# Fewer products on zeros at program begin, gate masks on GpSimd, diagonals and one V copy on VectorE

## The chip, the cores and the metric

One core of one Trainium2 chip. The metric is the device time of one execution in microseconds (us), lower is better. The profiled span leaves out some 1.75 us of it (for instance a span of 799.7 and a time of 801.38 for one execution).

## The reference

A layer-norm, an attention part in four segments of 512 rows, and a gated MLP over 2048 rows. Only the beginning of the first part matters here:

```python
x = A_x                                  # 1 x 2048 x 1024, bfloat16
h = x + A_ref(layernorm(x), wq, wk, wv, wo, beta)
h2 = h + B_ref(layernorm(h), w_in, w_sp, b_sp, w_out)

# inside A_ref, for each of 4 segments of 512 rows, 32 heads of width 32:
#   logits = q k^T * scale + causal mask; a_dot = softmax(logits) v
#   g = sigmoid(beta) per head; o = g * a_mem + (1 - g) * a_dot
#   M = M + phi(k)^T v; z = z + sum(phi(k))
```

## The kernel before

The kernel records operations for five engines and derives the semaphore waits from what each reads and writes. Each engine is given its own operations in the order recorded; loads are issued by SyncE in their order. The loads at the beginning:

```python
for tc in range(4):
    x_load(tc)                                  # 4 x 256 KB: the rows of segment 0
for i in range(0, 8, 2):                        # wv in four quarters of 256 KB
    sp.dma_start(WV[0][:, i:i + 2, :], A_wv[i * 128:(i + 2) * 128, 0:512]...)
sp.dma_start(WK[:, :, 0:256], ...)
sp.dma_start(WQ[:, :, 0:256], ...)
sp.dma_start(BETAB[:], A_beta.partition_broadcast(128))
sp.dma_start(WV[1][:], ...)
```

The first segment is normalised in a hurry: each tile of 128 rows is centred (its mean subtracted), transposed on TensorE, copied out of PSUM, and multiplied by the V weights; the row scale `RS0` is applied afterwards, when V is copied out of PSUM, and for Q and K by a product of ones with diagonal matrices (`DIAG`, a high and a low part). Until the first centred tile is there, TensorE multiplies zeros:

```python
def warm(k):
    for _ in range(k):
        pe.matmul(bank(7), IDENT[:], ETMP[:, 0, :], start=True, stop=True)   # ETMP is zero

def rstd0(tc):
    pool.tensor_tensor(RS0[tc][:], RS[tc][:, 0:1], MHALF[:], ALU.pow)
    pool.tensor_single_scalar(DIAG[0][:, tc, :], IDENT[:], RS0[tc][:], ALU.mult)

def diag_lo(tc):
    dve.scalar_tensor_tensor(DIAG[1][:, tc, :], IDENT[:], RS0[tc][:], DIAG[0][:, tc, :], ALU.mult, ALU.subtract)

warm(12)
act_mean(1)
var0(ln_stats(XCH[0]))
c0 = center(0, MV[0][:, 0:1], ALU.subtract)
c1 = center(1, MEAN[1][:])
pe_Th(0, c0, dve, dve)          # 8 transposes, two copies, both on VectorE
act_mean(2)                     # ACT: waits for x tile 2
pe_Th(1, c1, act, dve)          # 8 transposes, one copy on ACT, one on VectorE
# ... tiles 2 and 3 ...
warm(2)
for i in range(5):
    for t in range(2):
        v_mm(0, t, 0, vb[t], i)  # first V products: tiles 0 and 1 in turn, quarters of WV in order
# ...
mm8(bank(bk), lambda i: WK[:, i, 0:128], lambda i: XNT[0][:, i, :])
for i in range(2):
    pe.matmul(bank(br), ONES[:], DIAG[i][:]..., start=(i == 0), stop=(i == 1))
# ... rest of WK and WQ is loaded here (1.5 MB each) ...
gates()
phi_exp(0)
phi_max(0)                      # ends with a DMA transpose into PK
```

A quad is four heads. In the round of quad `n` TensorE does logits, projections of quad `n+1`, the products with V of quad `n-1`, and one product for the running state. The masks of the gates are made in the first round, on VectorE:

```python
def mask_g():
    dve.tensor_copy(MASKG[:, :, :, 0:32], GS[:]...to_broadcast([128, NQ, 4, 32]))
    for i in range(4):
        dve.tensor_single_scalar(MASKG[:, :, i, 0:32], MASKG[:, :, i, 0:32], BLK[:, i:i + 1], ALU.mult)
    for c in range(NQ):
        dve.tensor_copy(MASKG[:, c, :, 32], BLK[:])
# in the loop over rounds:  if n == 0: mask_g()
```

## Time and profile before

| | before |
|---|---|
| time, median of 3 | 802.42 us (802.40 to 802.46) |
| span of the profiled execution | 800.9 us |
| TensorE busy | 790.9 us |
| clock record at full speed from | 7.34 us |
| first V product | 8.41 us |
| first quarter of WV landed | 7.25 us |

The clock record is the trace's list of the clock granted to TensorE; in this trace products of 512 columns start 0.427 us apart before that instant and 0.216 us apart after it. "Landed" is the last of the 16 increments with which a load reports its parts.

The page's head and first part:

```profile
span 800.9 us, 12431 instructions
PE 790.9 (99%) x5304; PEld 380.8 (48%) x5374; DVE 380.5 (48%) x777; ACT 298.6 (37%) x348; POOL 127.3 (16%) x239
```

TensorE is the bound, so only what shortens its own order counts. The waits of TensorE in the first 34 us (what it waited for: us in total, times, longest):

```profile
PE ps L209 <- DVE ident L209: 1.7, 1, 1.7
PE ps L209 <- DVE rd L209: 0.5, 1, 0.5
PE ps L209 <- ACT e L209: 0.3, 2, 0.2
PE ps L209 <- issue: 0.2, 1, 0.2
```

("Issue" is time in which the profile shows nothing that was waited for.) The timeline of TensorE (start, us, engine, line, operation, output<-inputs, count, and in brackets the idle time before it with what ended it). Every operation has line 209, that of the recorder; one goes by tiles.

```profile
1.74 5.30 PE L209 MATMUL ps<-etmp,ident 128*128 128x512 bf16 x12 [1.74 <-DVE ident L209]
6.84 1.30 PE L209 MATMUL ps<-ident,lno 128*128 128x128 bf16 x16
7.98 0.59 PE L209 MATMUL ps<-etmp,ident 128*128 128x512 bf16 x2
8.41 2.32 PE L209 MATMUL ps<-wv,xnT 128*128 128x512 bf16 x10
...
16.21 0.59 PE L209 MATMUL ps<-diag,ones 128*128 128x512 bf16 x2
...
30.50 0.41 PE L209 MATMUL ps<-v,pk 128*128 128x132 bf16 x4
31.45 1.67 PE L209 MATMUL ps<-xnT,wq 128*128 128x512 bf16 x7 [0.54 <-DVE rd L209]
```

There is no idle bracket between 1.74 and 8.41: the products on zeros fill that time. At 31.45 there is one. VectorE's timeline says why it was late there, with 3.4 us on the masks:

```profile
25.44 0.72 DVE L209 COPY maskg<-gs 128x1024 f32<-128x1024 f32 x1
26.20 2.02 DVE L209 TENSOR_SCALAR maskg<-maskg,blk 128x256 f32<-128x256 f32 x4
28.25 0.67 DVE L209 COPY maskg<-blk 128x4 f32<-128x4 f32 x8
```

### The profile page before, as it was taken

How to read it: one execution, taken by the hardware profiler on the slowest of the kernel's cores; microseconds unless marked ns; L12 is line 12 of the kernel's file. 1: busy time of each engine (PE TensorE's matmuls, PEld its weight loads, DVE VectorE, ACT ScalarE, POOL GpSimd, SP SyncE). 2: the span in 40 equal slices, each digit the busy share in tenths (PEclk: the TensorE clock that was granted, in tenths of full speed). 3: DMA queues.
4: the chain of work that ended last, by engine and by line, in shares of the span. 5: the costliest groups of instructions: out<-in, count | busy, mean ns of one | idle time of the engine just before them, and what ended most of it. 6: DMA issues, size and time to landing. Idle time of an engine off the chain costs nothing.

```text
span 800.9 us, 12431 instructions
## 1 busy us (share of the span) xinstructions
PE 790.9 (99%) x5304; PEld 380.8 (48%) x5374; DVE 380.5 (48%) x777; ACT 298.6 (37%) x348; POOL 127.3 (16%) x239
## 2 busy tenths in 40 slices
PE   9999999999999999999999999999999999999998
PEld 4445445555444445455544444444444444444444
DVE  6875688569853774844562000063234323323432
ACT  5777877877778675133333333100000000000000
POOL 3443333233333331100131000000000000000000
PEclk9999999999999999999999999999999999999999
DMA  9672535353515324611117000650270153021003
GB/s 299 169 162 58 93 81 119 87 100 83 100 32 126 113 54 105 166 47 53 53 53 132 1 0 1 200 110 5 80 132 1 33 114 71 0 66 48 1 7 86
DMA packets 125000, 64.79 MB, mean 81 GB/s; under 512 B 94992, under 2 KB 113936, under 8 KB 124944
## 3 DMA queue, kind: packets, MB, share of 16 engines
q1 hardware_dynamic: 124944, 63.99, 33.3%
q8 instruction: 42, 0.69, 0.4%
q14 instruction: 14, 0.11, 0.0%
HBM read 32.51 MB, written 8.39 MB: 51 GB/s over the span
## 4 chain that ended last, share of the span: by engine, by line
PE 95%; DVE 4%; issue 1%; ACT 0%
PE ps L209 95%; DVE stats L209 1%; DVE maskg L209 0%; DVE ta L209 0%; DVE otok L209 0%; DVE hch L209 0%; DVE pqk L209 0%; ACT e L209 0%; DVE rd L209 0%; DVE lno L209 0%; DVE etmp L209 0%; DVE qk L209 0%; DVE mzb L209 0%; DVE rdm L209 0%; DVE msum L209 0%
## 5 line engine op out<-in xcount | busy, mean ns | idle before, releaser
L209 PE MATMUL ps<-wspT,z 128*128 128x512 bf16 x878 | 193.1, 379 | 0.9
L209 ACT ACTIVATE e<-ps 128x2048 bf16<-128x2048 f32 (+1 forms) x96 | 152.8, 1592 | 49.3 <-PE ps L209 48.8
L209 PEld LDWEIGHTS ps<-wspT,z 128*128 128x128 bf16 x896 | 87.7, 98 | 105.7
L209 DVE TENSOR_TENSOR tmpg<-ps,brow 128x512 f32<-128x512 f32 x56 | 38.7, 691 | 197.0 <-DMA brow<-in_B_b_sp_dram 105.5
L209 POOL TENSOR_SCALAR_AFFINE_SELECT e<-e 128x512 bf16<-128x512 bf16 x128 | 84.4, 671 | 185.4 <-ACT e L209 185.4
L209 PE MATMUL ps<-win,hnT 128*128 128x448 bf16 x512 | 98.3, 352 | 0.0
L209 PE MATMUL ps<-w_out,yT 128*128 128x512 bf16 (+2 forms) x453 | 96.9, 372 | 0.5
L209 PE MATMUL ps<-hnT,win 128*128 128x512 bf16 x439 | 96.2, 379 | 0.5
L209 PEld LDWEIGHTS ps<-win,hnT 128*128 128x128 bf16 x512 | 49.8, 98 | 46.3 <-issue 0.2
L209 PEld LDWEIGHTS ps<-w_out,yT 128*128 128x128 bf16 x462 | 44.7, 98 | 52.4
L209 PEld LDWEIGHTS ps<-hnT,win 128*128 128x128 bf16 x448 | 43.8, 98 | 52.8
L209 PE MATMUL ps<-xnT,wk 128*128 128x512 bf16 x256 | 60.8, 380 | 0.0
L209 PE MATMUL ps<-wv,xnT 128*128 128x512 bf16 x254 | 58.7, 379 | 0.2 <-issue 0.2
L209 ACT ACTIVATE z<-ps 128x448 bf16<-128x448 f32 x60 | 32.5, 543 | 69.4 <-PE ps L209 69.4
L209 PE MATMUL ps<-wo,oT 128*128 128x512 bf16 x254 | 57.6, 379 | 0.1
L209 ACT ACTIVATE z1T<-ps 128x512 bf16<-128x512 f32 x56 | 33.4, 597 | 63.3 <-PE ps L209 63.3
L209 PE MATMUL ps<-xnT,wq 128*128 128x512 bf16 x226 | 54.0, 379 | 2.1 <-DVE rd L209 0.5
L209 DVE TENSOR_TENSOR fin<-fin,ps 128x512 bf16<-128x512 bf16 (+2 forms) x33 | 22.2, 672 | 71.2 <-DMA fin<-out_dram 40.0
L209 DVE BATCH_NORM_STATS2 zst<-z 128x6 f32<-128x448 bf16 x64 | 38.9, 620 | 30.1 <-ACT z L209 30.1
L209 PEld LDWEIGHTS ps<-v,e 128*128 128x128 bf16 x1280 | 37.3, 96 | 9.1 <-issue 1.7
L209 DVE TENSOR_TENSOR yT<-tmpg,z1T 128x512 bf16<-128x512 f32 x56 | 38.8, 692 | 1.9
L209 PE MATMUL ps<-v,e 128*128 128x33 bf16 x1280 | 38.4, 177 | 0.0
(82 smaller groups left out, 577.1 us busy)
## 6 DMA issues: line engine op xcount, KB each, us to landing
xch<-in_A_x_dram SPq DMA_DIRECT2D x16, 256.0 KB, 3.3
xr<-in_A_x_dram SPq DMA_DIRECT2D x16, 256.0 KB, 3.4
out_dram<-hch SPq DMA_DIRECT2D x16, 256.0 KB, 2.5
fin<-out_dram SPq DMA_DIRECT2D x16, 256.0 KB, 2.8
out_dram<-fin SPq DMA_DIRECT2D x31, 128.0 KB, 1.7
win<-in_B_w_in_dram SPq DMA_DIRECT2D x4, 896.0 KB, 5.3
w_out<-in_B_w_out_dram SPq DMA_DIRECT2D x1, 3584.0 KB, 13.7
win<-in_B_w_in_dram SPq DMA_DIRECT2D x3, 1024.0 KB, 5.3
```

The lines of the kernel that those rows point to most:

```text
L209: ins = getattr(e, op.name)(*op.args, **op.kw)
```

## The change

The intent: three products on zeros fewer, so that the transposes start when the first centred tile is ready; the masks on GpSimd, so that VectorE is not late in the first round; the diagonals' high parts on VectorE, next to the low ones; one copy of V on VectorE, so that ACT's exponentials are not held up; beta loaded earlier, since the gates are now computed earlier.

```diff
     sp.dma_start(WK[:, :, 0:256], wcols(A_wk, 0, 256))
+    sp.dma_start(BETAB[:], A_beta.partition_broadcast(128))
     sp.dma_start(WQ[:, :, 0:256], wcols(A_wq, 0, 256))
-    sp.dma_start(BETAB[:], A_beta.partition_broadcast(128))
@@ mask_g
-        dve.tensor_copy(MASKG[:, :, :, 0:32], ...)
+        pool.tensor_copy(MASKG[:, :, :, 0:32], ...)
         for i in range(4):
-            dve.tensor_single_scalar(MASKG[:, :, i, 0:32], ...)
-        for c in range(NQ):
-            dve.tensor_copy(MASKG[:, c, :, 32], BLK[:])
+            pool.tensor_single_scalar(MASKG[:, :, i, 0:32], ...)
+        pool.tensor_copy(MASKG[:, :, :, 32], BLK[:].unsqueeze(1).to_broadcast([128, NQ, 4]))
@@ v_out
+        if (s, tcl, half) == (0, 3, 0):
+            dve.tensor_single_scalar(o, v, RS0[tcl][:], ALU.mult)
+        else:
+            act.activation(o, v, ACTF.Copy, scale=RS0[tcl][:] if s == 0 else 1.0)
@@ rstd0 and diag_lo
-        pool.tensor_single_scalar(DIAG[0][:, tc, :], IDENT[:], RS0[tc][:], ALU.mult)
-    def diag_lo(tc):
+    def diag(tc):
+        dve.tensor_single_scalar(DIAG[0][:, tc, :], IDENT[:], RS0[tc][:], ALU.mult)
         dve.scalar_tensor_tensor(DIAG[1][:, tc, :], ...)
@@ order
-    warm(12)
+    warm(9)
...
     proj_v(0, 2, 0)
+    gates()
+    mask_g()
     bk, bq, br = next_bank(), next_bank(), next_bank()
...
-    gates()
     phi_exp(0)
...
-        if n == 0:
-            mask_g()
```

More of the change, by code (lines that the diff above doesn't have):

```diff
@@ L426, in mask_g @@
     def mask_g():
-        dve.tensor_copy(MASKG[:, :, :, 0:32],
-                        GS[:].rearrange("p (c i) -> p c i", i=4).unsqueeze(3).to_broadcast([128, NQ, 4, 32]))
+        pool.tensor_copy(MASKG[:, :, :, 0:32],
+                         GS[:].rearrange("p (c i) -> p c i", i=4).unsqueeze(3).to_broadcast([128, NQ, 4, 32]))
         for i in range(4):
-            dve.tensor_single_scalar(MASKG[:, :, i, 0:32], MASKG[:, :, i, 0:32], BLK[:, i:i + 1], ALU.mult)
-        for c in range(NQ):
-            dve.tensor_copy(MASKG[:, c, :, 32], BLK[:])
+            pool.tensor_single_scalar(MASKG[:, :, i, 0:32], MASKG[:, :, i, 0:32], BLK[:, i:i + 1], ALU.mult)
+        pool.tensor_copy(MASKG[:, :, :, 32], BLK[:].unsqueeze(1).to_broadcast([128, NQ, 4]))
     lnc = [0]
@@ L475, in v_out @@
     def v_out(s, tcl, half, b):
-        act.activation(V[:, tcl, 16 * half:16 * half + 16, 0:32], bank(b).rearrange("p (h d) -> p h d", d=32),
-                       ACTF.Copy, scale=RS0[tcl][:] if s == 0 else 1.0)
+        o = V[:, tcl, 16 * half:16 * half + 16, 0:32]
+        v = bank(b).rearrange("p (h d) -> p h d", d=32)
+        if (s, tcl, half) == (0, 3, 0):
+            dve.tensor_single_scalar(o, v, RS0[tcl][:], ALU.mult)
+        else:
+            act.activation(o, v, ACTF.Copy, scale=RS0[tcl][:] if s == 0 else 1.0)
     def v_mm(s, tcl, half, b, i):
@@ L681, in bass_sequential_preLN__memory_aug_infini_attn__mixer_gmlp__prompt_kernel @@
     rstd0(2)
-    diag_lo(0)
+    diag(0)
     for i in range(5, 8):
@@ L687, in bass_sequential_preLN__memory_aug_infini_attn__mixer_gmlp__prompt_kernel @@
     v_out(0, 0, 0, vb[0])
-    diag_lo(1)
-    diag_lo(3)
-    diag_lo(2)
+    diag(1)
+    diag(3)
+    diag(2)
     v_out(0, 1, 0, vb[1])
     proj_v(0, 2, 0)
+    gates()
+    mask_g()
     bk, bq, br = next_bank(), next_bank(), next_bank()
```

## The prediction

> **What bounds it now.** TensorE is busy 790.9 of 800.9 us (page, busy times); 95% of the chain that ended last is TensorE. The change gains only what it takes out of TensorE's order before the steady state. In the timeline of 0 to 60 us three gaps do not recur:
>
> - Start: the first product on zeros starts at 1.74 us, the twelve follow every 0.427 us, the first transposes start at 6.83. The trace's clock record goes to full speed at 7.33: 512-column products are 0.427 us apart before, 0.216 after; transposes 0.107 and 0.056. The Trainium skill, "TensorE: Matmul & The Clock Gate", Part 1, gives these spacings (the trace agrees) and says that the window that opens the clock runs free and counts time, not products.
> - At 22.56 and 24.96 TensorE waits some 0.22 us each for ACT's exponentials (1.88 us) of quad 0.
> - At 31.45 the Q projection starts 0.71 us late, 0.22 in later rounds: 0.49 lost. It waits for VectorE's `qk`/`rd`, late because the gate masks take 3.4 us (25.44 to 28.9, VectorE's timeline).
>
> **The change, and its worth.**
>
> 1. Three products fewer: 3 x 0.427 = 1.28 us. The first centred tile is written at 5.63, so transposes start near 5.69, not 6.83. But if the clock still opens at 7.33, the 16 transposes now run cold (1.65 us; 1.14 before), and the first V product starts near 7.80, not 8.40. Worth 0.6. Quarters of WV land at 7.25, 8.09, 8.82, 9.59, needed from 7.8, 8.7, 9.5, 10.4.
> 2. Diagonals on VectorE. GpSimd's took 0.62 us each; the last diagonal ended at 16.10, TensorE used it at 16.20. Without this part the 0.6 would be lost there. VectorE needs about 0.25 + 0.35 us a pair (estimate from its low parts) and should end near 15.4; TensorE asks at 15.6. It protects (1), and is the tightest spot.
> 3. Masks on GpSimd: 3.4 us off VectorE; the 0.49 should vanish. GpSimd's affine select of 512 elements takes 0.65 us, so I estimate 3 to 6 us for 1024 + 4 x 256 + 32 elements, from 16.2 on. It idles until its selects (22.59), so nothing is held.
> 4. V copy on VectorE: ACT's second exponential started at 23.04, when its logits had just ended, so the copy hid in the wait. Worth about 0.
> 5. Beta ahead of WQ: 8 KB. WQ lands at 13.13, needed at 16.0. Worth 0.
>
> The DMA engines are saturated until about 28 us. The rest of WK lands at 24.7 (needed 26.7), the rest of WQ at 28.9 (needed 30.0), the first `pk` transpose at 29.3 (needed 29.8): little slack, but none should bind.
>
> **On the critical path:** 0.60 + 0.49 = 1.1 us; after 31 us every round takes 7.6 us of TensorE without a new wait, so the shift should reach the end. 802.42 - 1.1 = 801.3 us; 8 in 10: 800.6 to 801.9. Chances: faster by over 2% 0.01, within 2% 0.98, slower by over 2% 0.01.
>
> **What would show it.** (1) First V product near 7.8, first logits near 19.6 instead of 20.19, the clock record again at 7.3. (2) No wait before the `diag,ones` products. (3) The 0.71 spacing back to 0.22, GpSimd's masks over by 22 us. (4) ACT's exponentials at the same distance from the logits.
>
> **What would make it wrong.** The clock opens a window later (about 3.4 us) because the array idles at 5.6: loses up to 1.7 us. Or earlier: gains up to 1.2 instead of 0.6. Diagonals late, or VectorE and GpSimd slowing each other, would eat a few tenths. A load (rest of WQ, `pk`) that does not move earlier would cap the second gain.

## The result, and the profile after

Four executions of the changed kernel took 802.38, 801.76, 801.38 and 801.94 us, median 801.85; four of the kernel before on the same chip 802.40 to 802.46, median 802.43. The ratio is 0.9993, 95% interval 0.9976 to 1.001: the same. (Ratios are the mean time of one kernel's fast runs over that of the other's of the same rounds, so not quite the ratio of the medians quoted.) The median lies in the predicted range of 800.6 to 801.9, but only 0.05 us below its upper end, and two of the four executions lie above it; the gain is 0.6 us where 1.1 was forecast, and the changed kernel's executions differ by 1.0 us.

The profiled execution is the slowest of the four, 802.38 us. Its page, head and first part:

```profile
span 800.7 us, 12419 instructions
PE 789.3 (99%) x5301; PEld 380.0 (47%) x5371; DVE 379.2 (47%) x769; ACT 297.9 (37%) x347; POOL 129.0 (16%) x241
```

TensorE is busy for 1.6 us less, and the span is only 0.2 us shorter: it now waits. Its waits in the first 34 us:

```profile
PE ps L209 <- DVE ident L209: 1.7, 1, 1.7
PE ps L209 <- DMA wv<-in_A_wv_dram: 1.2, 1, 1.2
PE ps L209 <- DVE lno L209: 0.6, 1, 0.6
PE ps L209 <- ACT e L209: 0.3, 2, 0.2
```

Two waits are new; `rd` and the 0.2 us of "issue" are gone. Its timeline:

```profile
1.74 3.45 PE L209 MATMUL ps<-etmp,ident 128*128 128x512 bf16 x9 [1.74 <-DVE ident L209]
5.80 1.07 PE L209 MATMUL ps<-ident,lno 128*128 128x128 bf16 x16 [0.61 <-DVE lno L209]
6.70 0.59 PE L209 MATMUL ps<-etmp,ident 128*128 128x512 bf16 x2
8.51 2.32 PE L209 MATMUL ps<-wv,xnT 128*128 128x512 bf16 x10 [1.21 <-DMA wv<-in_A_wv_dram]
...
16.31 0.59 PE L209 MATMUL ps<-diag,ones 128*128 128x512 bf16 x2
...
30.78 0.41 PE L209 MATMUL ps<-v,pk 128*128 128x132 bf16 x4
31.24 1.67 PE L209 MATMUL ps<-xnT,wq 128*128 128x512 bf16 x7
```

The transposes start 1.04 us earlier than before, and the first V product 0.10 us later: it waits for the first quarter of WV, which landed at 8.37 us here and at 7.25 in the trace of before. The clock record reads full speed from 4.47 us, not 7.34. At 31.24 the bracket with `rd` is gone, as forecast. The masks on GpSimd took 5.6 us (16.35 to 21.97), inside the forecast, and GpSimd still idled before its first select:

```profile
16.35 1.05 POOL L209 COPY maskg<-gs 128x1024 f32<-128x1024 f32 x1 [2.00 <-DVE gs L209]
17.50 4.16 POOL L209 TENSOR_SCALAR maskg<-maskg,blk 128x256 f32<-128x256 f32 x4
21.73 0.24 POOL L209 COPY maskg<-blk 128x32 f32<-128x32 f32 x1
22.68 0.64 POOL L209 TENSOR_SCALAR_AFFINE_SELECT e<-e 128x512 bf16<-128x512 bf16 x1 [0.71 <-ACT e L209]
```

The chain of waits through the first 50 us (start, us, what) shows both loads that now hold TensorE. It runs through the quarter of WV, then TensorE, then the first transpose into `pk`:

```profile
2.65 5.72 DMA wv<-in_A_wv_dram
8.37 0.14 issue
8.51 3.63 PE ps L209 x22
...
20.49 10.24 DMA pk<-pqk
30.73 0.05 issue
30.78 0.41 PE ps L209 x4
```

The transpose's landing at 30.73 costs 0.20 us: the state products follow 0.53 us after the logits before them (30.25), where 0.33 us is usual (30.17 to 30.50 before).

So one theory was: **A**, the masks give a steady 0.5 us; the front's gain is uncertain, because the first V product starts at the later of two things that move from execution to execution, the landing of WV and the end of the transposes (which depends on when the clock opens). The rival was: **B**, the front gives its 0.6 in every run and the masks' gain is taken back by the late `pk` transpose or by GpSimd.

### The profile page after: what moved, and what is told of

The parts are those of the page before. It is cut to its first block, busy times and chain, and to the rows that moved or that the text cites. A ratio compares the mean times of both kernels' runs of the same rounds, so it can differ in the third digit from the quotient of the medians.

```text
span 800.7 us, 12419 instructions
## 1 busy us (share of the span) xinstructions
PE 789.3 (99%) x5301; PEld 380.0 (47%) x5371; DVE 379.2 (47%) x769; ACT 297.9 (37%) x347; POOL 129.0 (16%) x241
## 4 chain that ended last, share of the span: by engine, by line
PE 94%; DVE 3%; DMA 2%; issue 1%; SPq 0%
PE ps L209 94%; DMA pk<-pqk 1%; DMA wv<-in_A_wv_dram 1%; DVE stats L209 1%; DVE ta L209 0%; DVE otok L209 0%; DVE hch L209 0%; SPq L209 0%; DVE rd L209 0%; DVE pqk L209 0%; DVE mzb L209 0%; DVE lno L209 0%; DVE rdm L209 0%; DVE msum L209 0%; DVE mv L209 0%
```

## The experiments

Twelve kernels, all correct. For each, the trace was read for the same few points. "End minus second V" is the span minus the start of the second V product, that is, all the rest of the kernel.

| run | zeros | masks | first quarter of WV | clock opens | first V | second V | end minus second V | mean time |
|---|---|---|---|---|---|---|---|---|
| before | 12 | VectorE | 7.25 | 7.34 | 8.41 | 8.62 | 792.26 | see below |
| after | 9 | GpSimd | 8.37 | 4.47 | 8.51 | 8.72 | 791.94 | 801.87 |
| k1_after_again | 9 | GpSimd | 7.58 | 7.28 | 7.72 | 7.94 | 791.72 | 801.68 |
| k2_nine_only | 9 | VectorE | 7.96 | 4.57 | 8.10 | 8.31 | 792.24 | 802.11 |
| k3_rest_only | 12 | GpSimd | 7.72 | 7.36 | 8.42 | 8.63 | 791.74 | 801.94 |
| k4_masks_only | 12 | GpSimd | 7.74 | 6.91 | 8.21 | 8.42 | 791.76 | 801.87 |
| k5_wv_first | 9 | GpSimd | 6.14 | 7.43 | 7.90 | 8.60 | 791.76 | 801.80 |
| k6_wv_first_twelve | 12 | GpSimd | 6.01 | 7.54 | 8.42 | 9.23 | 791.77 | 802.26 |
| k7_wv_first_split | 9 | GpSimd | 6.03 | 5.15 | 7.25 | 8.45 | 791.76 | 802.12 |
| k8_wv_first_pool_diag | 9 | GpSimd | 5.98 | 5.20 | 7.10 | 8.46 | 791.76 | 801.93 (one run) |
| k9_copy_on_dve | 9 | GpSimd | 6.40 | 6.17 | 7.28 | 7.53 | 791.92 | 801.36 |
| k10_copy_twelve | 12 | GpSimd | 5.66 | 5.67 | 7.59 | 7.83 | 791.90 | 801.56 |
| k11_copy_old_order | 9 | GpSimd | 7.85 | 7.12 | 7.99 | 8.20 | 792.40 | 801.76 |
| k12_copy_pool_diag | 9 | GpSimd | 6.17 | 5.85 | 7.11 | 7.35 | 792.52 | 801.55 |

Points of time are from the span's start and from one execution each (the landings and the clock are the trace's records of them); the times are means of 4 or 5 executions. Beside them the kernel before ran nine times in each of three groups (k1 to k4, k5 to k8, k9 to k12; three chips): means 802.23, 802.32 and 802.16, single runs 801.57 to 802.94. The three runs within 0.06 us that the prediction had started from were luck (the profiled execution of that kernel took 802.64). Every interval of a ratio reaches 0.0012 to 0.0016 to each side and holds 1, so the times alone settle nothing under 1 us; the traces have to.

### The changed kernel once more

Edit: a comment.

> The changed kernel once more, only a comment added. Theory A (the front gain is uncertain: the first V product starts at the later of the landing of the first quarter of WV and the end of the transposes, and both move from run to run; the gain of 0.5 us at the masks is steady): times again spread by about 1 us, between 801.3 and 802.4, median near 801.8; in the profile the first V product starts within 0.15 us of the later of the two. Rival B (the front gives its 0.6 us in every run and the masks' 0.5 us is taken back by the late landing of the first pk transpose or by GpSimd): spread below 0.2 us, and the profiled run that showed an 8.51 start was a stray.

Measured: 801.29 to 802.44, median 801.64; ratio 0.9994 (0.998 to 1.0007). The spread is A's. The clock opened at 7.28 in this trace, close to the 7.34 that the prediction assumed, and the front came out as the prediction had it: first V product at 7.72 (forecast 7.80), first logits at 19.50 (forecast 19.6), end minus second V 0.54 us less than before. Here the landing plus 0.14 (7.72) and the instant 0.216 us after the start of the last zero product (also 7.72) coincide.

### Nine products alone, everything else alone, masks alone

```diff
 k2_nine_only, against before
-    warm(12)
+    warm(9)
 k3_rest_only, against after
-    warm(9)
+    warm(12)
 k4_masks_only, against before: mask_g on GpSimd as in the change, and
     proj_v(0, 2, 0)
+    gates()
+    mask_g()
...
-    gates()
     phi_exp(0)
...
-        if n == 0:
-            mask_g()
```

> The kernel before with nine products on zeros and nothing else changed. Theory A: gain of 0 to 0.6 us with a spread of 0.5 us or more, median near 802.2, since the wait for WV or the last diagonal on GpSimd takes part of it. Rival B: a steady 801.8 (gain 0.6), spread below 0.2 us. A third outcome, no gain at all (802.4) with TensorE waiting before the diag,ones products at about 16.1, would say that the diagonals on VectorE were needed for any front gain.

> The changed kernel with twelve products on zeros again. Theory A: the masks' gain alone, 801.9 to 802.0, and as narrow a spread as the kernel before has (0.1 us), since the twelve products hide the landing of WV and the clock. Rival B: about 802.3, and the spacing before the Q projection near 31 us is not back at 0.22 us.

> The kernel before with the gates early and the gate masks on GpSimd, nothing else. Theory A: 801.9 to 802.0, spread 0.1 us, the same as the kernel with everything but the nine products. Rival B: 802.3 to 802.4.

Measured: nine products alone, mean 802.11 against 802.23 of before (ratio 0.9998, 0.9986 to 1.0011). Everything but the nine products, 801.94 (0.9996, 0.9983 to 1.0009). Masks alone, 801.87 (0.9995, 0.9983 to 1.0008).

- **Masks.** End minus second V falls into two groups: 792.24 and 792.26 with the masks on VectorE, 791.72 to 791.77 with them on GpSimd in every trace without another wait. The difference, 0.50 us, is what the prediction had (0.49). B falls: its steady front is not there, and the masks' gain stays; only the late `pk` transpose, which B named, took a part of it in single traces (0.20 us in `after`).
- **Diagonals, V copy, beta.** k3 has them, k4 has not; their end minus second V is 791.74 and 791.76. With the front where it is in these runs they are worth nothing.
- **Nine products.** In k2 the quarter of WV landed at 7.96 and the first V product came at 8.10, though the zero products had ended at 7.16. The profile puts the wait down to VectorE's centring of a tile, which these products do not read; the landing record 0.14 us before shows what it was. (ACT's copy of tile 1 ended at 7.96 as well, but the first V product does not read it: in k5, below, it starts 0.65 us before that copy ends.)

```profile
5.67 1.07 PE L209 MATMUL ps<-ident,lno 128*128 128x128 bf16 x16 [0.43 <-DVE lno L209]
6.57 0.59 PE L209 MATMUL ps<-etmp,ident 128*128 128x512 bf16 x2
8.10 1.24 PE L209 MATMUL ps<-wv,xnT 128*128 128x512 bf16 x5 [0.93 <-DVE lno L209]
```

- **A's forecast of a narrow spread with twelve products was wrong**: k3 ran from 801.17 to 802.86. Twelve products do not hide the clock: it opened anywhere from 4.47 to 7.54 us in these fourteen traces, and the earlier it opens the earlier the twelve end (first V product at 8.42 in k3, 8.21 in k4, 7.59 in k10, with the clock at 7.36, 6.91, 5.67). Only one execution of k3 was traced, so what made up its 1.7 us of spread is not shown.

### WV ahead of two tiles of x

```diff
-    for tc in range(4):
-        x_load(tc)
-    for i in range(0, 8, 2):
-        sp.dma_start(WV[0][:, i:i + 2, :], ...)
+    x_load(0); x_load(1); wv_load(0); x_load(2); wv_load(2); x_load(3); wv_load(4); wv_load(6)
```

k5 is the changed kernel with this; k6 has `warm(12)` as well; k7 loads the rest of WQ in two parts, the second (columns 512 on) after `phi_max(0)`; k8 puts the diagonals' high parts back on GpSimd.

> The changed kernel with the first two quarters of WV issued ahead of the x tiles 2 and 3 (order x0 x1 q0 x2 q1 x3 q2 q3). Theory A (the nine products gain nothing because the first quarter of WV lands too late, at 7.6 to 8.4, and the first V product follows the landing by 0.14 us): the quarter lands near 6.2 to 6.8, the first V product starts right after the second pair of zero products, at 6.7 to 7.8 by where the clock opens, and the span is that start plus 791.95 us, so 400 to 1200 ns shorter than the changed kernel's mean of 801.75: 800.6 to 801.3; unless the first pk transpose or the rest of WQ, which land near 29 to 30.7 by DMA alone, become the wait. Rival C (the front is limited by the centred x tiles or the copies, not by WV): the first V product does not start earlier than 7.7, time 801.7.

> The same load order, with twelve products on zeros. Theory A: the first V product again starts where the twelve products and the transposes let it, 8.2 to 8.5 when the clock opens near 7, earlier only if it opens earlier; so about 0.5 us slower than the same order with nine, 801.5 to 802.0. Rival C: no difference from the nine.

> The load order of the run before last, nine products, and the rest of WQ in two parts, the second issued after the first pk transpose. Theory A: the first pk transpose lands near 25 to 26 instead of 29 to 30.7, so no wait before the first state product, and the front's gain reaches the end in full: 0.1 to 0.4 us below the unsplit order, 800.4 to 801.1. If the pk landing never bound, no difference.

> The new load order with nine products, and the high parts of the diagonals on GpSimd as before. My prediction said that the diagonals on VectorE protect the front's gain: then TensorE waits 0.3 to 0.8 us before the diag,ones products (they start over 7.80 us after the first V product, where all runs so far have 7.79 to 7.80). Rival: GpSimd's chain moves forward with the front, as in the run with nine products alone, and the distance stays 7.80.

Measured: k5 801.80 (ratio 0.9993, 0.998 to 1.0005), no better than the changed kernel; k6 802.26 (0.9996, 0.9981 to 1.0012); k7 802.12 (0.9996, 0.9984 to 1.0009); k8 801.93, one run. A's forecast failed in part: WV's first quarter did land at 6.0 to 6.1 and the first V product did start at once (7.10 to 7.90 with nine), but the second did not follow. In k5, TensorE:

```profile
7.90 0.38 PE L209 MATMUL ps<-wv,xnT 128*128 128x512 bf16 x1
8.60 2.12 PE L209 MATMUL ps<-wv,xnT 128*128 128x512 bf16 x9 [0.32 <-ACT xnT L209]
```

and ACT:

```profile
6.91 1.06 ACT L209 ACTIVATE junk<-xch 128x1024 bf16<-128x1024 bf16 x1 [1.59 <-DMA xch<-in_A_x_dram]
7.87 0.19 ACT L209 ACTIVATION_READ_ACCUMULATOR junk<-xch 128x1 f32 x1
7.97 0.58 ACT L209 ACTIVATE xnT<-ps 128x512 bf16<-128x512 bf16 x1
```

The second V product needs ACT's copy of tile 1, and in ACT's order that copy stands behind the mean of x tile 2, which waits for its load, moved back by the new order. One load's delay was traded for another's. Rival C named the copies, so it was half right: two limits lay close together. Splitting WQ (k7) made the `pk` transpose land at 26.51 instead of 28.6 to 28.9 and won nothing, since here the state products came no earlier than 30.3. (k7's mean is 0.3 us above k5's; its trace shows no wait that explains it.) In k8 the `diag,ones` products start 7.59 us after the second V product, the distance of all the other traces so far (7.58 to 7.59): with this front, diagonals on GpSimd cost nothing.

### The copy of tile 1 on VectorE

```diff
 k9_copy_on_dve, against k5
-    pe_Th(1, c1, act, dve)
+    pe_Th(1, c1, dve, dve)
```

k10 is k9 with `warm(12)`; k11 is the changed kernel (old load order) with this edit alone; k12 is k9 with the diagonals' high parts on GpSimd.

> The load order with WV first and nine products; the copy of tile 1's first half out of PSUM moved from ACT to VectorE. In the four runs with the new order the second V product waited for this copy (0.3 to 1.1 us after the first), because ACT does the mean of x tile 2 first and that tile now lands later. Theory A (every start-up gain ends at the later of three things: clock and transposes, first quarter of WV, copies of tiles 0 and 1; span is the start of the second V product plus 791.75): the second V product follows the first by 0.22 to 0.4 us, at 7.2 to 8.2, so the span is 799.0 to 799.9 and the time 800.7 to 801.6, about 0.5 below the changed kernel. If the quarters of WV or tile 2's centring bind next, the later V products show it. Rival: no change from the run with the copy on ACT (801.8), the second V product still at 8.4.

> The same with twelve products on zeros. Theory A: with WV and the copy out of the way, the products' number now decides: with a clock that opens at 7.3 the second V product comes at 8.6, so 0.6 us later than with nine; with a clock at 4.5 to 5.2 the difference is 0.1 or none. On the mean 0.3 to 0.6 us slower than with nine, 801.4 to 802.0. Rival (the zero products cost nothing in any case): equal to nine.

> The changed kernel with only that copy moved to VectorE, loads in the old order. Theory A: the first quarter of WV still lands at 7.5 to 8.4 and the first V product still follows it by 0.14 us: 801.7, no gain over the changed kernel. Rival (the copy alone was the limit): 801.2 with the second V product before the landing's time would allow in the other runs, near 7.5.

> New load order, nine products, copy on VectorE, and the diagonals' high parts on GpSimd as in the kernel before. My prediction's step 2 (diagonals on VectorE protect the front's gain): the diag,ones products start more than 7.59 us after the second V product, by 0.2 to 0.7 us, and the time is higher by that than with the diagonals on VectorE. Rival (GpSimd's chain moves with the front): 7.59 again, time equal.

Measured: k9 801.20 to 801.60, mean 801.36, against 802.16 of before in the same rounds (801.81 to 802.66); ratio 0.9991, 0.9978 to 1.0003. It has the lowest mean, and no overlap of single times with the kernel before beside it, though the interval of the ratio just holds 1. The changed kernel itself was not run beside it. The second V product comes at 7.53:

```profile
5.78 1.23 PE L209 MATMUL ps<-ident,lno 128*128 128x128 bf16 x16 [0.16 <-DVE lno L209]
6.85 0.59 PE L209 MATMUL ps<-etmp,ident 128*128 128x512 bf16 x2
7.28 2.51 PE L209 MATMUL ps<-wv,xnT 128*128 128x512 bf16 x10
```

- **What is left in k9:** its end minus second V is 0.16 above the usual. The third quarter of WV landed at 9.14, and the V product that needs it started at 9.19, 0.14 late. That is the next limit.
- **k10, twelve products:** 801.56 (0.9993, 0.9981 to 1.0006), 0.20 above k9, in the direction of A and below its 0.3 to 0.6. In its trace the clock opened at 5.67, and the second V product came 0.30 later than in k9. The traces had different clocks, so this is one sample of the products' worth, not their mean. (Its end minus second V holds 0.15 us of the `pk` wait, landing at 29.81.)
- **k11, old order:** 801.76 (0.9993, 0.9978 to 1.0009), no gain over the changed kernel, as A had it. WV landed at 7.85, the first V product came at 7.99; the last copy ended at 7.94, so here the two limits coincide. Its end minus second V is 0.65 us above the others: the `pk` transpose landed at 30.66 and held the state products, in the profile a wait of 0.58 us for that load:

```profile
30.71 0.41 PE L209 MATMUL ps<-v,pk 128*128 128x132 bf16 x4 [0.58 <-DMA pk<-pqk]
```

- **k12, diagonals on GpSimd:** 801.55 (0.9993, 0.9979 to 1.0007), 0.19 above k9. The `diag,ones` products start 8.16 us after the second V product instead of 7.58. Of these 0.58, 0.27 arise in the V products (the third quarter of WV again; one spacing is 0.47 instead of 0.22), and 0.31 are the wait for the first diagonals. The second of the two products then comes 0.39 after the first instead of 0.22, so the Q projection behind them starts 0.49 us late for the diagonals' sake. TensorE's weight loads show it, the first for GpSimd's high part, the second for VectorE's low part:

```profile
15.51 0.10 PEld L209 LDWEIGHTS ps<-diag,ones 128*128 128x128 bf16 x1 [0.64 <-POOL diag L209]
15.90 0.10 PEld L209 LDWEIGHTS ps<-diag,ones 128*128 128x128 bf16 x1 [0.29 <-DVE diag L209]
```

So step 2 of the prediction is right for this front and load order (second V product at 7.35). Part of that is the load order: x tile 3 landed at 8.2 to 8.3 in k8 and k12 and at 6.5 to 7.7 in the old order, and the last low part of the diagonals, with the high parts on GpSimd, was ready at 15.84 in k12, 15.52 in k8, but at 15.24 in k2.

## Why the prediction was right or wrong

The time was inside the range and "within 2%" was right; that the median fell inside by 0.05 us is in part luck, since the central forecast, 801.3, was missed by half of the forecast gain. The sum was 0.60 + 0.49; it measured about 0.5 in all: the changed kernel's nine times average 801.76, the 31 of the kernel before 802.26 (over several chips, so a rough figure).

- **Step 3, the masks: right, in mechanism and size.** The wait at 31.45 vanished; 0.50 us against 0.49. GpSimd took 5.6 us (estimated 3 to 6) and held up TensorE nowhere. The prediction's worry that VectorE and GpSimd slow each other did show, off TensorE's path: beside the masks on GpSimd, VectorE's operation `pqk<-pqk,etmp` took 0.59 us in `after`, against 0.43 in `before`, where GpSimd was idle then. And in `before` two of VectorE's four multiplications of the masks took 0.60 us while GpSimd was at its selects, and the two after them 0.35, so some 0.5 us of the 3.4 (an estimate from these four; not tested) came from that.
- **Step 1, the nine products: the term that was mis-sized, 0.6 forecast.** Four pairs of kernels differ in nine or twelve alone, and their means by 0.12 (k2 and before), 0.25 (k1 and k3, before rounding), 0.46 (k5 and k6) and 0.20 us (k9 and k10): 0.26 on the mean. The single times of each pair overlap (standard deviations of one kernel's times 0.10 to 0.62 us), and the last two pairs have another load order, so for the changed kernel the times alone leave the worth open between none and the forecast 0.6 (the first two pairs: 0.19 on the mean, with two standard errors of 0.4). The traces give a figure more directly, if from few executions: in the seven of the old load order the first V product starts at 8.08 on the mean with nine products (7.72 to 8.51) and at 8.35 with twelve (8.21 to 8.42), so 0.27 us earlier. Two assumptions failed. "Quarters of WV land at 7.25, 8.09, 8.82, 9.59, needed from 7.8, 8.7, 9.5, 10.4" took one trace's landings for fixed: in the seven traces of the old load order the first quarter landed between 7.25 and 8.37, and in `after` and in k2 the first V product followed that landing by 0.14 us, at 8.51 and 8.10, long after the transposes. And "if the clock still opens at 7.33" took one trace's clock for fixed: it opened between 4.47 and 7.54. When it opens early, twelve products cost less as well (each takes 0.216 and not 0.427 us), so there is less to save. The prediction had put up to 1.2 us on an early clock; in `after` the clock was early (4.47), and the wait for WV took it all. In k1, where the clock opened as assumed and WV, though later than assumed (7.58), was still in time, the forecast front came true to 0.1 us.
- **Step 2, the diagonals: not needed for the gain that came.** "Without this part the 0.6 would be lost there" is not what k2 and k8 show: with GpSimd's diagonals, the second V product at 8.31 and 8.46, no wait. GpSimd's own chain moved forward with the front. At 7.35 (k12) it cost 0.49. For the front that the prediction had in mind, a second V product near 8.0, no run tried it; such a front asks for the diagonals near 15.6, and k2 had them at 15.24, so by an estimate from k2 they would not have bound there either.
- **Steps 4 and 5, the V copy and beta: right as far as tested.** ACT's second exponential starts 0.45 us after the logits (22.66 to 23.11), before 0.47; and k3 and k4 differ by 0.02.
- **"Little slack, but none should bind":** wrong for the `pk` transpose, which cost 0.20 us in the profiled execution, 0.15 in k10 and about 0.65 in k11. Under "what would make it wrong" it was named.
- **Left open:** what sets the instant at which the clock opens, and why the slowest of the 16 parts of the first WV quarter arrives between 7.25 and 8.37. No run controlled either. On the clock the traces say a little more: in all fourteen, the stretch at full speed lasted either 791.89 us (five) or 795.30 us (nine), which differ by 3.41 and are 232 and 233 times 3.4133, while the spans ran from 799.4 to 801.0. So the clock opens and closes in steps of 3.41 us, and how these steps lie to the start of the program differs from execution to execution.

## What to carry to other kernels

Time that is filled with dummy work hides waits: before removing it, ask what becomes the last condition without it, and take the spread of that condition over several executions, not its value in one trace. When the gain is smaller than the scatter of a start-up, split the span at the first dependent instruction; here everything after it was constant to 0.05 us for given masks, apart from waits that each trace names, and what the total times could not tell the two parts told at once. Relieving one start-up limit (WV) only shows the next (ACT's copy, then WV's third quarter or the `pk` transpose), so they have to be moved together.

## What the Trainium skill lacked or had wrong

- "TensorE: Matmul & The Clock Gate", Part 1, puts the opening at around 4 us into sustained activity, plus or minus 500 ns. It also says that the 3.4 us window runs free and that the number of slow products varies from run to run, which fits better. Here the clock opened 2.7 to 6.0 us after the first product (4.47 and 7.54 us, with first products at 1.74 and 1.59): a spread of 3.2 us, as a free window of 3.4 would give, not one of 1 us; the steps of 3.41 us (above) are such a window. The spacings of the page (0.427 and 0.216 us at 512 columns) agree with the traces.
- "GPSIMD Engine Reference", section 4.1 Engine selection, calls one-input work on GpSimd roughly line-rate. The copy of 1024 float32 fits (1.05 us; VectorE 0.72), but multiplying 256 float32 by a per-partition scalar took 0.97 us on the mean, nearly four times as long per element as the copy (VectorE 0.35 us, and 0.60 while GpSimd was at its selects; its copy, too, ran beside them).
- "DMA: Bandwidth & Descriptors", section "Why a DMA increments its semaphore by 16 and not by 1", says that only the full 16 means that all data landed. The traces agree, and add how much this can cost at a start: in `after` the first of the 16 increments of the first WV quarter came at 6.59 us and the last at 8.37. No page gives the spread from execution to execution of a landing under load (7.25 to 8.37 for the same transfer, in seven traces).
